# Reordering the head of a fused Fourier mixing and two-layer kernel: a forward piece, a table part, the layer weights and one copy

## Chip, core and metric

The kernel runs on one core of one Trainium2 chip. The metric is the device time of one execution in microseconds (us); 775.15 us is the median of three runs of the kernel before (773.96 to 775.66). The profile is of one further execution.

The engines are named as the profile names them: PE is TensorE (matmuls; PEld its weight loads), DVE is VectorE, ACT is ScalarE, POOL is GpSimd, SP is SyncE, which here only issues DMAs.

## What is computed

```python
def _attn_ref(x, filt_r, filt_i):            # x: (8, 3008, 256), filters: (1505, 256)
    X = np.fft.rfft(x, axis=1)
    F = (filt_r + 1j * filt_i)[None, :, :]
    y = np.fft.irfft(X * F, n=x.shape[1], axis=1)
    return y

def _moe_ref(x, w_in, w_out, alpha):         # x: (24064, 256), w_in: (256, 2048), w_out: (2048, 256)
    h = x @ w_in
    g = np.maximum(h, 0.0) + alpha * np.minimum(h, 0.0)
    return g @ w_out

def reference(x, filt_r, filt_i, w_in, w_out, alpha):
    y = _attn_ref(x, filt_r, filt_i)
    return _moe_ref(y.reshape(24064, 256), w_in, w_out, alpha)
```

Along the sequence each of the eight batches is filtered in the Fourier domain; then every token goes through two dense layers with a leaky activation whose slope differs by hidden unit.

## The kernel before

**Two halves woven together.** The length 3008 is split as 94 x 32. Each batch's transform is a chain of matmul stages (forward over 94, forward over 32, filter product, inverse over 32, inverse over 94) whose result is written to `yT`, channels on partitions and tokens along the free dimension. The dense layers work on blocks of 512 tokens (one of 384 in each pair of batches): `Block.up` multiplies `win_s` by `yT` into PSUM (L547), ScalarE copies it to `gtb` (L556), VectorE applies the activation (L559, L561), and `Block.down` multiplies by `wout_s` (L601). While the layers of one batch run, the transforms of the next are laid between them by a hand-written plan of steps. Sixteen steps make a block.

**The order is the program's.** The kernel's scheduling is manual: each engine takes its instructions in the order in which the code writes them, and an instruction that waits holds up all that stands behind it on its engine. The order around the change is therefore the order of the lines below.

**The first batch (class `First`, L412 to L512)** has nothing to run beside, so it has stages of its own, without trips through DRAM:

- `piece_a` (eight): forward over 94, into `am`.
- `turn_at(kp, n, evict)`, here "array piece kp": matmuls against the identity that transpose `am` into the array `at` for the products kp to kp + n - 1 (L343). They go to a bank pair of `psF` (or of `psH` with `wide`) and are copied out by the engine `evict` (the copies of all helpers on ScalarE and VectorE carry the lines L305 and L308).
- `piece_b(kp)`, twelve, the "forward pieces": 16 small matmuls (L355) of `twf_s` and `at` into a bank pair of `psH`, then one VectorE product with the filter (L360) into `uu`. Forward piece kp reads what the array piece that covers kp has left.
- `piece_c(kp)`, twelve: 16 matmuls (L382) of `uu` with the inverse tables `twi_s` and `twx_s` into two banks of `psO`; a pair of pieces shares the two banks. `keep_c` copies a pair out to `v` by ScalarE.
- `half_t`, `piece_t` (L399): transpose `v` into `zt`; `half_d`, `pair_d` (L283): the inverse over 94, into `psO` or `psF`, copied to `yT`. A `pair_d` fills a bank pair of `psF`.

**PSUM.** The pools `psH` and `psO` have two buffers each and `psF` has one (L77 to L79), so a stage that writes to `psF` waits until the last content of `psF` has been copied out.

**Tables.** `twf_s` comes in three parts of eight columns by SP's queue (`table`, L417; the second and third wait for a VectorE memset each). `inverse_table(ka, pb)` transposes one part with four matmuls (L421) into the bank `pb`, and ScalarE copies it to `twi_s`. `swapped(ka, eng)` makes `twx_s` from it (L428, L429): VectorE for part one, POOL for parts two and three. Pieces C 0 to 3 read part one, 4 to 7 part two, 8 to 11 part three.

**Warm matmuls.** `warm(n, pw)` issues n matmuls of 128x512 with the identity (L438) whose result nobody reads.

**Loads on POOL's queue.** The filters of the first batch (L140), in three groups, then the layer weights `win_s` (L482, two transfers) and `wout_s` (L485), with the inputs `xs` of the second batch between (L118). In front of the `win_s` load stands a VectorE memset of two of its columns (L480). The load waits for the memset, and the memset stands in VectorE's order behind the filter product of a certain piece; so its place in the loop sets when the load is issued.

**The first block (from L700)** runs in 16 steps: `up4(i, half)` in the even ones (L570: eight matmuls for four hidden groups and 256 tokens into one `psH` buffer; L578: ScalarE's copy; with half 1 also VectorE's activation L583, L584), and what is left of the first batch between, put into the plan step by step (L653 to L664). In step 0, `up4` also has the slopes of the activation and two copies done.

Of the kernel before, what the change touches and what calls it, by code (L numbers as in the profile page):

```python
# [51 lines left out]
def kernel(  # L52
# [10 lines left out]
    nc = tc.nc  # L63
# [48 lines left out]
    def load_x(b, c, held=False):  # L112
        xs = p_x.tile([128, 8 * D], FP16, name="xs")
        if held:
            for r in (slice(0, 32), slice(64, 96)):
                nc.vector.memset(xs[r, 0:2], 0.0)
        for r in (slice(0, 48), slice(48, N1)):
            nc.gpsimd.dma_start(out=xs[r], in_=xrow(b, c)[r])  # L118
        return xs
# [25 lines left out]
    def banks(wide):  # L145
        if wide:
            return psH.tile([128, 2, 512], FP32, name="hps")
        return psF.tile([128, 2, 512], FP32, name="psF")

    def bank(kind):  # L150
        if kind == "o":
            return psO.tile([128, 2, D], FP32, name="op").rearrange("p k d -> p (k d)")
        return banks(kind == "h")[:, 0]
# [150 lines left out]
    def on_act(o, i):  # L304
        nc.scalar.activation(o, i, AF.Copy)  # L305
# [113 lines left out]
    def inverse_table(ka, pb):  # L419
        for i in range(4):  # L420
            nc.tensor.matmul(pb[:, 128 * i : 128 * i + 128],  # L421
                             twf_s[:, ka + 2 * i : ka + 2 * i + 2].rearrange("p k m -> p (k m)"), id16,
                             start=True, stop=True)
        on_act(twi_s[:, ka : ka + 8].rearrange("p k m -> p (k m)"), pb)

    def swapped(ka, eng):
        t, o = twi_s[:, ka : ka + 8], twx_s[:, ka : ka + 8]
        eng.tensor_scalar(o[:, :, 32:64], t[:, :, 0:32], gs_s, None, OP.mult)  # L428
        eng.tensor_scalar(o[:, :, 0:32], t[:, :, 32:64], gs_s, -1.0, OP.mult, OP.mult)  # L429

    xc = {(0, c): load_x(0, c) for c in range(4)}
    f0 = First()
# [3 lines left out]
    def warm(n, pw):  # L436
        for _ in range(n):
            nc.tensor.matmul(pw.rearrange("p (r c) -> p r c", r=4), id16,  # L438
                             id16.unsqueeze(1).to_broadcast([128, 4, 128]), start=True, stop=True)
# [24 lines left out]
    swapped(8, nc.gpsimd)  # L464
    load_filt(nc.gpsimd, filt_s, 8, 12, (1,))
    f0.piece_b(1)
    warm(2, bank("o"))
    f0.turn_at(4, 2, on_act)
    nc.sync.dma_start(out=wi3_s, in_=consts["wi3"].ap())
    nc.sync.dma_start(out=al16, in_=moe_alpha.rearrange("(j p) -> j p", p=128))  # L470
# [3 lines left out]
    for r in (slice(0, 64), slice(64, 128)):  # L474
        nc.sync.dma_start(out=wfq_s[r], in_=consts["wfq"].ap()[r])
    for kp in range(12):
        if kp < 10:
            f0.piece_b(kp + 2)
        if kp == 5:
            nc.vector.memset(win_s[:, :, 0:1], 0.0)  # L480
            for kt in range(2):
                nc.gpsimd.dma_start(out=win_s[:, kt], in_=moe_w_in[kt * 128 : (kt + 1) * 128])  # L482
            xc[(1, 0)] = load_x(1, 0)
            for q in range(2):
                nc.gpsimd.dma_start(  # L485
                    out=wout_s[:, 8 * q : 8 * q + 8],
                    in_=moe_w_out[1024 * q : 1024 * q + 1024].rearrange("(j p) d -> p j d", p=128))
            for c in range(1, 4):
                xc[(1, c)] = load_x(1, c)
        f0.piece_c(kp)  # L490
        if kp > 9:
            f0.keep_c(kp, (on_act, on_act) if kp == 10 else both, 1)
        elif kp % 2 == 1:
            f0.keep_c(kp - 1, (on_act, on_act))
            if kp < 7:
                f0.turn_at(kp + 5, 2, on_act)
        if kp == 0:
            inverse_table(16, banks(False)[:, 0])
            swapped(16, nc.gpsimd)
        if 7 < kp < 10:  # L500
            warm(2, banks(False)[:, 0])
    for o in range(0, 128, 64):
# [109 lines left out]
    def put(step, fn, *args):  # L612
        plan.setdefault(step, []).append((fn, args))
# [42 lines left out]
    for i in (6, 7):  # L656
        put(3, lambda i=i: on_dve(*f0.half_t(i, "o")))
    put(5, f0.pair_d, 2, on_dve)
    put(9, f0.pair_d, 3, on_act)
    for g, ts, ds, te, de in ((2, (19, 23), (25, 28), (on_dve, on_dve), (on_dve, on_dve)),  # L660
                              (3, (32, 34), (43, 49), (on_act, on_act), (on_act, on_act))):
        for i in range(2):
# [102 lines left out]
```

## Time and profile before

| | |
|---|---|
| median of three runs | 775.15 us (773.96 to 775.66) |
| the profiled execution's own time | 773.89 us |
| its span, first to last instruction | 772.1 us |
| TensorE busy | 761.2 us, 99% |
| VectorE / ScalarE / POOL busy | 633.4 / 583.9 / 148.2 us |
| granted TensorE clock | 1.00 |
| DMA | 99.77 MB, mean 129 GB/s |

The profile's times are us from the span's start. A group's line reads: start, length, engine, line, operation, output<-input, shape, count, and in brackets the idle time of the engine before it with what ended it. Groups with a count span several instructions. TensorE by stretches:

| us | TensorE busy | what runs |
|---|---|---|
| 0 to 16 | 13.24 of 16.00 | loads, `piece_a`, warm matmuls |
| 16 to 20 | 3.56 of 4.00 | first array pieces and forward pieces |
| 20 to 27 | 6.59 of 7.00 | loop over the pieces, first half |
| 27 to 32 | 4.36 of 5.00 | loop, second half |
| 32 to 36.1 | 2.95 of 4.10 | last stages up to the first `yT`, start of the layer |
| 36.1 to 42 | 5.89 of 5.90 | first block, first part |
| 42 to 49 | 5.91 of 7.00 | first block, second part |
| 49 to 60 | 11.00 of 11.00 | second block with the second batch's transform |

Some matmul records can be missing from a trace, and the ends of matmuls are modelled.

### The profile page before, as it was taken

The page shows a single profiled execution, that of the slowest core. Times are in us where ns is not written, and L with a number is a line of the kernel's source. Part 1 is how long each engine was busy: PE and PEld are TensorE (multiplying, and loading weights), DVE is VectorE, ACT ScalarE, POOL GpSimd, SP SyncE. Part 2 cuts the span into 40 slices and gives each one's busy share as a digit, 9 for nine tenths or more (in the row PEclk, how much of TensorE's full clock was granted, in tenths as well). Part 3 has the DMA queues.
Part 4 walks back from the last instruction along what each step waited for, and adds up shares of the span by engine and source line. Part 5 has one row for each costly group of instructions (what it writes and reads, how often), then busy time and mean ns, then how long its engine had stood idle before and what let it go on. Part 6 is the DMA issues. An engine that isn't in the chain of part 4 may idle for free.

```text
span 772.1 us, 16602 instructions
## 1 busy us (share of the span) xinstructions
PE 761.2 (99%) x6552; PEld 510.5 (66%) x6552; DVE 633.4 (82%) x1159; ACT 583.9 (76%) x672; POOL 148.2 (19%) x278
## 2 busy tenths in 40 slices
PE   8899999999999999999999999999999999999998
PEld 4576656666666666666666666766666666766666
DVE  3788885889898998899978998899877888666663
ACT  3677788888778787887778878787777777676664
POOL 7620660132202212121201222022111112000000
PEclk9999999999999999999999999999999999999999
DMA  9896797674854548724783438644473233510111
GB/s 162 129 226 179 132 202 193 176 161 127 193 137 107 131 121 172 192 71 104 183 223 87 115 101 175 185 103 110 119 159 103 65 77 96 152 36 28 42 42 56
DMA packets 96814, 99.77 MB, mean 129 GB/s; under 512 B 12020, under 2 KB 83076, under 8 KB 96544
## 3 DMA queue, kind: packets, MB, share of 16 engines
q1 hardware_dynamic: 82048, 69.22, 32.5%
q0 software_dynamic: 14688, 29.49, 21.5%
q8 instruction: 51, 0.84, 0.5%
q14 instruction: 27, 0.22, 0.1%
HBM read 54.74 MB, written 46.66 MB: 131 GB/s over the span
## 4 chain that ended last, share of the span: by engine, by line
PE 95%; ACT 2%; DMA 1%; issue 1%; DVE 0%; POOL 0%; DVEq 0%; ACTq 0%
PE op L601 42%; PE hps L547 41%; PE psF L283 3%; PE hps L261 2%; PE psF L230 1%; PE op L438 1%; PE hps L176 1%; DMA win_s<-in_moe_w_in_dram 1%; PE hps L202 1%; ACT asb L305 1%; PE hps L570 1%; ACT gtb L578 1%; PE psF L399 0%; ACT gtb L556 0%; DVE uu L360 0%
## 5 line engine op out<-in xcount | busy, mean ns | idle before, releaser
L556 ACT ACTIVATE gtb<-hps 128x1024 f16<-128x1024 f32 (+1 forms) x376 | 377.4, 1006 | 134.7 <-PE hps L547 130.9
L601 PE MATMUL op<-wout_s,gtb 128*128 128x256 f16 x3008 | 431.3, 273 | 0.0
L547 PE MATMUL hps<-yT,win_s 128*128 128x512 f16 (+1 forms) x1504 | 418.4, 375 | 0.9 <-ACT asb L305 0.3
L601 PEld LDWEIGHTS <-gtb 128*128 128x128 f16 x3008 | 291.0, 98 | 164.2 <-issue 10.7
L559 DVE TENSOR_SCALAR m<-gtb,alm_s 128x512 f16<-128x512 f16 (+1 forms) x752 | 227.1, 345 | 99.6 <-ACT gtb L556 98.2
L561 DVE TENSOR_TENSOR gtb<-gtb,m 128x2048 f16<-128x2048 f16 (+1 forms) x188 | 226.1, 1203 | 10.3
L547 PEld LDWEIGHTS <-win_s 128*128 128x128 f16 x1504 | 142.6, 98 | 55.2 <-issue 6.6
L244 POOL DMA_DIRECT2D sw<-ww x144 | 71.6, 506 | 414.6 <-DVE ww L237 408.9
L606 ACT ACTIVATE osb<-op 128x512 f32<-128x512 f32 (+1 forms) x97 | 56.6, 584 | 12.4 <-PE op L601 11.3
L305 ACT ACTIVATE asb<-hps 128x1024 f16<-128x1024 f32 (+1 forms) x56 | 56.6, 1020 | 5.6 <-PE hps L176 4.3
L305 ACT ACTIVATE v<-hps 128x1024 f16<-128x1024 f32 (+1 forms) x43 | 43.4, 1010 | 10.8 <-PE hps L261 10.6
L237 DVE TENSOR_TENSOR ww<-psF,filts_s 128x1024 f16<-128x1024 f32 x42 | 51.2, 1218 | 0.2 <-PE psF L230 0.2
L238 DVE TENSOR_TENSOR uu<-psF,filt_s 128x1024 f16<-128x1024 f32 x42 | 51.0, 1215 | 0.0
L305 ACT ACTIVATE yT<-psF 128x752 f16<-128x752 f32 x59 | 46.9, 796 | 2.0 <-PE psF L283 1.9
L283 PEld LDWEIGHTS <-zt 96*128 96x128 f16 x512 | 28.6, 98 | 6.0 <-issue 0.3
L283 PE MATMUL psF<-wi_s,zt 96*128 96x94 f16 x496 | 31.0, 205 | 0.1
L242 POOL DMA_DIRECT2D uu<-ww x24 | 19.6, 1255 | 32.7 <-DVE uu L238 24.7
L249 DVE TENSOR_TENSOR uu<-uu,sw 128x1024 f16<-128x1024 f16 x36 | 24.6, 683 | 1.2 <-DMA sw<-ww 0.9
L118 POOL DMA_DIRECT2D xs<-in_x_dram x32 | 21.6, 889 | 13.1 <-PE hps L547 4.8
L186 DVE TENSOR_TENSOR xs<-xs 47x2048 f16<-47x2048 f16 x16 | 19.5, 1219 | 0.4
L190 DVE TENSOR_TENSOR xs<-xs 47x2048 f16<-47x2048 f16 x16 | 19.4, 1210 | 0.0
L261 PE MATMUL hps<-uu,twi_s 64*64 64x256 f16 x336 | 17.3, 281 | 0.0
(88 smaller groups left out, 264.4 us busy)
## 6 DMA issues: line engine op xcount, KB each, us to landing
out_dram<-osb SPq DMA_DIRECT2D x128, 128.0 KB
v_dram<-v SPq DMA_DIRECT2D x84, 128.0 KB
zt<-v_dram SPq DMA_DIRECT2D x28, 384.0 KB
sw<-ww POOLq DMA_DIRECT2D x144, 64.0 KB, 2.8
xs<-in_x_dram POOLq DMA_DIRECT2D x44, 192.0 KB, 6.4
at<-a_dram SPq DMA_DIRECT2D x40, 192.0 KB
a_dram<-asb SPq DMA_DIRECT2D x32, 192.0 KB
a_dram<-asb SPq DMA_DIRECT2D x12, 384.0 KB
```

The lines of the kernel that those rows point to most:

```text
L237: nc.vector.tensor_mul(ww, px, fs)
L238: nc.vector.tensor_mul(uu, px, f)
L244: nc.gpsimd.dma_start(out=sw[o : o + 32], in_=ww[i : i + 32])
L261: nc.tensor.matmul(ps[64 * par : 64 * par + 64, e, 256 * h : 256 * h + 256], twi_s[r, 4 * q + 2 * h + par], u[r, par, h], start=True, stop ...
L283: nc.tensor.matmul(ps[:, m], self.zt[:, 8 * g + 4 * mh + m, dh * 128 : dh * 128 + 128], wi3_s, start=True, stop=True)
L305: nc.scalar.activation(o, i, AF.Copy)
L547: nc.tensor.matmul(self.hps[:, j % 2, 0:tn], win_s[:, kt, j * 128 : (j + 1) * 128], yT[:, kt, self.t0 : self.t0 + tn], start=(kt == 0), st ...
L556: nc.scalar.activation(g[:, 2 * i : 2 * i + 2], self.hps[:, :, 0:tn], AF.Copy)
L559: nc.vector.tensor_scalar(m[:, 2 * i + h], g[:, 2 * i + h], 0.0, a, OP.min, OP.mult)
L561: nc.vector.tensor_add(g, g, m)
L601: nc.tensor.matmul(self.op[:, si - s0], self.gts[k][:, 128 * si : 128 * si + 128], wout_s[:, k], start=(si == s0 and k == 0), stop=(si == ...
L606: nc.scalar.activation(osb[:, 0:m], self.op[:, 0:m], AF.Copy)
```

## The change

Four places, all in the first 50 us.

- In the head, the two warm matmuls behind forward piece 1 are taken out. In their place stand `inverse_table` and `swapped` for table part three, with a bank of `psO` in place of one of `psF`, and then forward piece 2. Array piece 4 follows these. In the loop, piece 2 and the table part are taken out.
- In the loop, the memset and the six POOL loads behind it (two of `win_s`, `xs`, `wout_s`, `xs`) stand in round 4 in place of round 5: behind forward piece 6, not 7.
- `pair_d` 3 of the first batch stands in step 7 in place of step 9, and VectorE copies it in place of ScalarE.

```diff
@@ -464,7 +464,9 @@
     swapped(8, nc.gpsimd)
     load_filt(nc.gpsimd, filt_s, 8, 12, (1,))
     f0.piece_b(1)
-    warm(2, bank("o"))
+    inverse_table(16, bank("o"))
+    swapped(16, nc.gpsimd)
+    f0.piece_b(2)
     f0.turn_at(4, 2, on_act)
     nc.sync.dma_start(out=wi3_s, in_=consts["wi3"].ap())
     nc.sync.dma_start(out=al16, in_=moe_alpha.rearrange("(j p) -> j p", p=128))
@@ -474,9 +476,9 @@
     for kp in range(12):
-        if kp < 10:
+        if 0 < kp < 10:
             f0.piece_b(kp + 2)
-        if kp == 5:
+        if kp == 4:
             nc.vector.memset(win_s[:, :, 0:1], 0.0)
             for kt in range(2):
                 nc.gpsimd.dma_start(out=win_s[:, kt], in_=moe_w_in[kt * 128 : (kt + 1) * 128])
@@ -494,9 +496,6 @@
             f0.keep_c(kp - 1, (on_act, on_act))
             if kp < 7:
                 f0.turn_at(kp + 5, 2, on_act)
-        if kp == 0:
-            inverse_table(16, banks(False)[:, 0])
-            swapped(16, nc.gpsimd)
         if 7 < kp < 10:
             warm(2, banks(False)[:, 0])
@@ -656,7 +655,7 @@
     put(5, f0.pair_d, 2, on_dve)
-    put(9, f0.pair_d, 3, on_act)
+    put(7, f0.pair_d, 3, on_dve)
```

## The prediction

> **What bounds the kernel now.** I read four views in this order. First the page's busy table, and TensorE's waits over the whole span, longest total first (us in total, times, longest):
>
> ```profile
> PE 761.2 (99%) x6552; PEld 510.5 (66%) x6552; DVE 633.4 (82%) x1159; ACT 583.9 (76%) x672; POOL 148.2 (19%) x278
> ...
> PE hps L570 <- DMA win_s<-in_moe_w_in_dram: 0.8, 1, 0.8
> PE hps L570 <- ACT gtb L578: 0.6, 1, 0.6
> ...
> PE psF L421 <- ACT at L305: 0.4, 1, 0.4
> PE hps L570 <- ACT yT L305: 0.4, 1, 0.4
> ```
>
> TensorE is busy 761.2 of 772.1 us. Split by window, this view lists only two waits after 80 us, 0.2 us each (a PSUM copy near 117 us, another near 149), and the stretch 49 to 60 has 11.00 of 11.00 us busy. So from 49 us on the time is TensorE's own work, and a microsecond saved before that should come off the end whole. All four edits act before 49 us.
>
> Second, the chain of waits over the first 60 us (start, length, what):
>
> ```profile
> 18.96 1.03 ACT at L305
> ...
> 20.03 0.38 PE psF L421 x4
> ...
> 27.07 0.43 POOL win_s L482
> ...
> 27.66 8.41 DMA win_s<-in_moe_w_in_dram
> ...
> 36.11 0.94 PE hps L570 x7
> ```
>
> The chain runs through an array copy by ScalarE, the third table part, the filter products (L360), then the load of `win_s`, which VectorE's memset releases. It lands at 36.06 and the first layer product goes on at 36.11.
>
> Third, VectorE in order of time, which shows how products and memset stand:
>
> ```profile
> 16.72 2.36 DVE L360 TENSOR_TENSOR uu<-hps,filt_s 128x1024 f16<-128x1024 f32 x2 [0.21 <-DMA filt_s<-in_filt_r_dram]
> 19.34 1.22 DVE L360 TENSOR_TENSOR uu<-hps,filt_s 128x1024 f16<-128x1024 f32 x1 [0.26 <-PE hps L355]
> 20.83 7.05 DVE L360 TENSOR_TENSOR uu<-hps,filt_s 128x1024 f16<-128x1024 f32 x6 [0.27 <-PE hps L355]
> 26.70 0.06 DVE L480 MEMSET win_s<- 128x2 f16 x1
> ```
>
> Products 0 and 1 end at 19.08; VectorE then idles 0.26 us for piece 2 and 0.27 for piece 3. Products 4 to 7 start at 22.12, 23.26, 24.39 and 25.55 by the chain: 1.15 us apart.
>
> Fourth, TensorE around the start of the layer:
>
> ```profile
> 35.09 0.27 PE L570 MATMUL hps<-yT,win_s 128*128 128x256 f16 x1 [0.41 <-ACT yT L305]
> 36.11 0.94 PE L570 MATMUL hps<-yT,win_s 128*128 128x256 f16 x7 [0.76 <-DMA win_s<-in_moe_w_in_dram]
> ```
>
> Without the load's wait the second matmul would follow the first by its 0.11 to 0.13 us, at 35.20. So the load costs 36.11 - 35.20 = 0.91 us, and whatever is gained beyond that must come from the FFT chain that makes `yT` ready at 35.09.
>
> **Piece 2 and table part 3 moved.** Removed from the head: the two warm matmuls at 17.70 (0.54 us of TensorE). In their place stand the table's four (0.22 us, row at 20.03), to 17.92. Piece 2 reads what the array copy of 17.24 to 18.26 leaves, so it cannot start before about 18.31 (it was 18.85); its 16 matmuls take 0.34. Array piece 4 follows at 18.65, 0.34 later than before, its copy from 19.30 to 20.33 instead of 18.96 to 19.98. ScalarE's table copy (0.60) now stands ahead of it, from 18.68 to 19.28, in time in which ScalarE waits for array piece 4 anyway; without that cover it would add its 0.6 to the array copy. Two things wait on these copies. Piece C 0 needs both `psO` banks, and the second is now the table's: free at 19.28, so C 0 at 19.33 (19.20 before). Array piece 6 needs `psF`, free at 20.33.
>
> From there: piece 3 at 19.70 instead of 20.35, because the 0.43 us wait for `psF` and the table's 0.32 have left the loop. Product 2 follows product 1 directly (19.08), product 3 starts at 20.25 (20.83 before), array piece 6 at 20.38, piece 4 at 20.95, product 4 at 21.37 against 22.12: 0.75 us sooner. The loop behind (C, copies of C, array piece) keeps its 2.25 us per pair, within VectorE's 2.3. I take 0.7 sooner for the whole FFT chain; the bounds are 0.26 (only the idle before product 2 goes) and 0.75. Filters don't hold it: those for products 4 to 7 were issued by 17.09 and landed within 4.6 us, r parts by 18.9 and i parts by 20.1; the last ones, for 8 to 11, landed at 25.5 (issued 23.0, 2.5 us), and product 8 would start at about 26.0. POOL's order is unchanged: the swapped copy of part 3 stays behind the last filter issue, 23.60 to 24.99, and layer weights come next. SP's queue is not touched.
>
> Is part 3 of `twf_s` there at 17.7? The trace shows its issue at 13.00 and a first reader at 20.03 that waited for ScalarE, not for it. SP's queue has by its packet count (81,664 left at 13.0 us, 81,338 at 15.5; 256 are the two last table parts) moved it by 15.5. So landing lies between 15.5 and 20.03. I take the early end, no cost; the late end is a rival below.
>
> **Layer weights one product sooner.** The memset moves from behind product 7 to behind product 6: 1.15 us. With the 0.75 of product 4 it comes at 24.80 instead of 26.70. POOL finishes its swapped copy at 24.99 and then issues six transfers, `win_s` first: 25.2 instead of 27.07. The DMA rows say 0.10 busy share in 25 to 26 and 0.00 in 26 to 28, so the load meets nothing, and takes its 9.0 us from issue to landing: 34.2. Lower bound, from one product alone: 36.06 - 1.15 = 34.91. The issues of `xs` and `wout_s` behind it shift with it; each is wanted later (`wout_s` at 47.2).
>
> First layer matmul: 35.09 - 0.7 = 34.4, the second at 34.5, the load at 34.2 no longer last. Gain: 36.11 - 34.5 = **1.6 us**, of which 0.9 is the load and 0.7 the FFT. Bounds: 36.06 - 34.91 = 1.15 if the load stays last, 0.91 + 0.26 = 1.17 if the FFT hardly moves, 0.91 + 0.75 = 1.66 at best.
>
> **One copy on VectorE, a step earlier.** In the chain:
>
> ```profile
> 42.28 1.94 ACT gtb L578 x2
> 44.21 0.69 ACT yT L305
> 44.90 0.93 ACT gtb L578
> ```
>
> ScalarE loses 0.69 there. But pair 3 now stands ahead of the layer's fifth product, and its bank `psF` is free only when VectorE has copied pair 2, at 42.34. Times of before: pair 3 at 42.39 to 42.80, fifth product until 43.7, its copy from 43.75 instead of 43.22: 0.53 given back, so 0.16 left, of which I take 0.1. On VectorE the copy (0.94, as pair 2) falls into an idle stretch of 1.90 us before 44.25; what is late next is the activation of the first chunk, by 0.53, and VectorE then runs without idle until 58.7. The nearest consumer is pair 4, which TensorE starts at 59.41 and which needs VectorE's copy ending at 58.67: 0.7 us of slack, just enough. Bounds: +0.69 saved to 0.55 lost.
>
> **Sum.** 1.6 + 0.1 = 1.7 us off. The profiled execution was 773.89 us (span 772.1 and 1.8 around it), so 772.2; it lies 1.26 below the median shown, and from the median 775.15 I forecast **773.45 us**, 0.22% less. Own range of this case: 1.2 to 2.4 off.
>
> **Rivals.** (1) Load or FFT moves only half way: 0.9 to 1.2 off, **774.1**. For it: piece 2 still waits for an array copy, and slacks in the loop (piece 4 ends 21.3, VectorE wants it 21.35) are near nothing. Against: no new wait is longer than the one removed. 11%. (2) VectorE becomes the bound from 44 us: 0.55 lost instead of 0.1 gained, 1.6 - 0.55 = 1.05 off, **774.1**. For: no idle until 58.7. Against: the 0.7 of slack. 8%. (3) Table part 3 lands late, at its bound of 20.03. TensorE stops at the head of its queue, with piece 2, array piece 4 and C 0 behind it; product 2 then starts at 20.66, product 4 at 23.3, 1.2 later than before, and the layer at 36.3: 0.3 slower, **775.4**. Against: the packet count. 4%. (4) The other side: the TensorE clock. The warm matmuls leave a hole of 0.4 us at 17.9. If the granted clock fell to half from there for about 4 us, the 3.56 us of work that the rows show busy in 16 to 20 would take as much again; TensorE would be last in the loop, 3.6 - 1.7 = 1.9 us more than before, **777.0**. It decides from a mean clock below about 0.7 in that stretch. Against: 1.00 in every row, also in 32.0 to 36.1, where TensorE is busy only 2.95 of 4.10 us. 13%, with whatever else I have not seen on that side.
>
> [...]
>
> **How the numbers follow.** Forecast 64%. About 0.2% (1.55 us) is what a measurement of this kernel can tell from no change; the forecast's 1.7 is barely beyond it, and I put 57 of its 64 there and 7 within. Rivals 1 to 3 fall within (23). So faster 0.57, same 0.30, slower 0.13. The range holds the forecast and rivals 1 to 3 and the spread of runs (773.96 to 775.66, 0.85 to each side): 772.3 to 775.9; it leaves rival 4 out.
>
> **What would show it.** Right: no idle before product 2; product 4 near 21.4; memset near 24.8 and `win_s` issued near 25.2; first two layer matmuls 0.1 apart near 34.4; the block's first L547 at 47.2 instead of 48.92; span 770.4. Wrong: TensorE waiting at 17.7 for `twf_s`; a wait for the load still there; clock below 1.00 in 16 to 22; a new wait for VectorE near 57 us; or the lead at 49 us lost again later.

## The result

The changed kernel takes 772.56 us (median of seven runs, 772.30 to 773.03) against 775.15 us (seven runs, 773.96 to 775.66): a ratio of 0.9972, 95% interval 0.996 to 0.9983, or 2.59 us at the medians. The profiled execution took 772.30 us with a span of 770.5 us, 1.6 us less than the span of before. The forecast was 773.45 us with a span of 770.4.

TensorE's waits after the change, longest total first, without the one for the very first load (us in total, times, longest). Lines behind the change carry numbers one lower than before: L569 is the first block's layer product, L546 that of the later blocks.

```profile
PE hps L546 <- ACT asb L305: 0.5, 2, 0.3
PE hps L569 <- ACT yT L305: 0.4, 1, 0.4
...
PE hps L569 <- ACT gtb L577: 0.2, 1, 0.2
PE hps L355 <- ACT at L305: 0.2, 1, 0.2
```

The wait for `win_s` (0.8) and the wait for `psF` ahead of the table (0.4) are gone; the one for ScalarE's layer copies fell from 0.6 to 0.2. New are three waits of 0.2 each: of forward piece 2 for the array copy, of a later forward piece for a product, and of pair 3 for VectorE's copy of pair 2.

VectorE and POOL after the change, groups in order of time:

```profile
16.84 9.16 DVE L360 TENSOR_TENSOR uu<-hps,filt_s 128x1024 f16<-128x1024 f32 x8 [0.49 <-DMA filt_s<-in_filt_r_dram]
24.81 0.06 DVE L482 MEMSET win_s<- 128x2 f16 x1
```

```profile
25.18 1.14 POOL L484 DMA_DIRECT2D win_s<-in_moe_w_in_dram  x2 [0.61 <-DVE win_s L482]
```

The first eight products now run without a hole; memset and load stand 1.9 us earlier than before (26.70 and 27.07).

TensorE after the change:

```profile
17.55 0.40 PE L421 MATMUL op<-ids,twf_s 128*128 128x128 f16 x4
18.16 0.41 PE L355 MATMUL hps<-at,twf_s 64*32 64x256 f16 x16 [0.22 <-ACT at L305]
...
34.20 1.16 PE L569 MATMUL hps<-yT,win_s 128*128 128x256 f16 x8 [0.40 <-ACT yT L305]
...
47.15 1.02 PE L546 MATMUL hps<-yT,win_s 128*128 128x512 f16 x4 [0.32 <-ACT asb L305]
```

All eight matmuls of the first layer product are one group: in this execution nothing waits for the weights. (In the profiles of f2 and g4 below, which have the same order of loads, a wait of 0.20 and 0.23 us is left, so the load still lands close to the moment at which it is wanted.) The second block starts at 47.15 instead of 48.92, 1.77 us sooner; the span shows 1.6 of it, and where the other 0.17 went is told below.

### The profile page after: what moved, and what is told of

It is laid out like the page before. It is cut to its first block, busy times and chain, and to the rows that moved or that the text cites. A ratio compares the mean times of both kernels' runs of the same rounds, so it can differ in the third digit from the quotient of the medians.

```text
span 770.5 us, 16598 instructions
## 1 busy us (share of the span) xinstructions
PE 760.9 (99%) x6550; PEld 510.2 (66%) x6550; DVE 634.2 (82%) x1160; ACT 583.2 (76%) x671; POOL 147.9 (19%) x278
## 3 DMA queue, kind: packets, MB, share of 16 engines
q0 software_dynamic: 14688, 29.49, 21.4%
## 4 chain that ended last, share of the span: by engine, by line
PE 96%; ACT 3%; issue 0%; DVE 0%; DMA 0%; ACTq 0%
PE op L600 42%; PE hps L546 41%; PE psF L283 3%; PE hps L261 2%; PE psF L230 1%; PE hps L176 1%; PE op L438 1%; PE hps L202 1%; ACT asb L305 1%; PE hps L569 1%; ACT v L305 1%; PE op L382 1%; PE psF L399 0%; ACT gtb L577 0%; ACT gtb L555 0%; PE hps L355 0%
## 5 line engine op out<-in xcount | busy, mean ns | idle before, releaser
L546 PE MATMUL hps<-yT,win_s 128*128 128x512 f16 (+1 forms) x1504 | 418.4, 375 | 0.9 <-ACT asb L305 0.5
L546 PEld LDWEIGHTS <-win_s 128*128 128x128 f16 x1504 | 142.5, 98 | 55.2 <-issue 6.6
```

Source lines behind the costliest of these rows:

```text
L546: nc.tensor.matmul(self.hps[:, j % 2, 0:tn], win_s[:, kt, j * 128 : (j + 1) * 128], yT[:, kt, self.t0 : self.t0 + tn], start=(kt == 0), st ...
```

## The experiments

Two things were open. Which part brings how much; and why the medians moved by 2.6 us where the two profiles differ by 1.6. The runs of before lie in two groups, 774.0 to 774.2 and 775.1 to 775.7, those after the change in one. Each run below has a mean granted TensorE clock on record; the tables count the runs at 0.998 or less, and the others are called undisturbed. Kernels named e were run on one chip, those named f on a second, those named g on a third, each set beside 33 runs of the kernel before on its own chip.

**Each part alone, and the change without its last part.**

```diff
 e1_head_only: of the change, only
+    inverse_table(16, bank("o")); swapped(16, nc.gpsimd); f0.piece_b(2)    # for warm(2, ...)
 e2_weights_only: of the change, only
-        if kp == 5:
+        if kp == 4:
 e3_copy_only: of the change, only
-    put(9, f0.pair_d, 3, on_act)
+    put(7, f0.pair_d, 3, on_dve)
 e4_no_copy: the change, but for e3's line
```

> Only piece 2 and table part 3 are moved; the layer weights stay behind product 7, pair 3 stays on ScalarE in step 9. Theory (the later of two ends sets the layer's start: yT from the FFT chain, or the load of the weights): the FFT chain alone makes the first layer matmul start at 34.2 (35.09 before), but product 7 ends near 26.0, so the weights are issued near 26.3 and land near 35.3; TensorE waits about 1.0 us for them, and 0.75 us of the 1.6 us of span is gained: span 771.3. Rival A (the weights' earlier issue is worth nothing by itself, the FFT chain brings all): no wait for the load, span 770.5. Rival B (the spread of the runs before, 773.96 to 775.66 in two groups 1.3 us apart, comes from the load's landing while it is last): this kernel still waits for the load, so its runs keep a spread above 1 us; if the spread comes from the head of the FFT instead, its runs lie within 0.8 us as those after the change do.

> Only the memset and the loads behind it are moved from product 7 to product 6; the head stays as before, pair 3 stays on ScalarE in step 9. Theory: weights issued 1.1 us sooner, near 25.95, landing near 34.95; first layer matmul stays at 35.09 and the second follows it at once, so 0.9 us is gained at the layer's start: span 771.2, and TensorE's wait for the load is gone. Rival A: the span stays at 772.1 because the load takes longer when it starts earlier. Rival B (spread from the load's landing): runs within 0.8 us, median below 774.2.

> Only pair 3 is moved to step 7 and copied by VectorE. Theory: of the 0.69 us that ScalarE saves about 0.53 is given back, since the fifth layer product now stands behind pair 3, which waits for its PSUM bank: 0.1 to 0.2 us sooner at the start of the second block (48.7 to 48.8, 48.92 before), span 771.9 to 772.0. Rival A: ScalarE's 0.69 come off whole, 48.2 and span 771.4. Rival B: VectorE becomes the bound, a wait for VectorE at 47 to 59 us and span 772.4 or more.

> The change without its last part: pair 3 stays in step 9 on ScalarE. Theory: the layer starts at 34.2 as after the change, the second block 0.1 us later than after it (47.25 against 47.15), span 770.6. Rival A: 0.5 to 0.7 us later (47.7 or more, span 771.1), if the copy on ScalarE costs more once the layer starts sooner. Rival B: sooner than after the change, if the copy's move only costs.

| kernel | runs | of them with clock 0.998 or less | median us | median of the others | ratio, 95% interval |
|---|---|---|---|---|---|
| before | 33 | 16 | 774.71 | 774.17 | |
| e1_head_only | 11 | 6 | 774.77 | 773.57 | 0.9999, 0.9988 to 1.0009 |
| e2_weights_only | 11 | 0 | 773.15 | 773.15 | 0.9976, 0.9967 to 0.9984 |
| e3_copy_only | 11 | 5 | 774.57 | 774.38 | 0.9998, 0.9988 to 1.0008 |
| e4_no_copy | 11 | 5 | 772.97 | 772.50 | 0.9987, 0.9976 to 0.9999 |

The groups are groups by clock. Where the weights come sooner alone, no run has the lower clock, and nearly the whole gain of the medians is there: 1.56 us, against 1.74 in e4, which has the head as well. The head and the copy alone measure as no change. Among undisturbed runs the head is worth more: 0.60 us alone (five runs, 0.75 expected) and 0.65 beside the weights (773.15 to 772.50); in e4 the runs with the lower clock give most of that back at the median. The profile of e1_head_only has a stretch at half clock. Windows of it (us, then busy us and count of TensorE, its weight loads, VectorE, ScalarE and POOL, granted clock, DMA share, GB/s):

```profile
33.69:37.10 3.41, 2.01 (x22) 1.29 (x20) 1.31 (x3) 1.27 (x3) 0.84 (x2) 1.00 1.17 195
37.10:40.50 3.40, 3.40 (x28) 2.92 (x26) 1.94 (x3) 1.39 (x3) 1.13 (x3) 0.51 1.45 198
40.50:44.00 3.50, 3.50 (x42) 3.14 (x41) 2.23 (x3) 2.61 (x3) 0.63 (x2) 0.99 1.18 217
```

The wait for the load (1.0 us here) and the one for `yT` (0.4) leave TensorE 2.01 of 3.41 us busy; then it runs at half clock for 3.4 us, in the first block, where it is the bound. The profile of e3_copy_only shows the same from 37.7 to 41.1. That suggests that my reading in the expectations, by which the spread comes from the load's landing time, missed the means, and that the wait brings the clock down; f3 below tests it.

For e2_weights_only, the chain of waits shows the first layer product in one piece:

```profile
34.64 1.16 PE hps L570 x8
```

Weights issued at 25.48 (25.95 expected), no wait for them, span 770.9 (771.2 expected). In this profile product 0 began 0.45 us sooner than in that of before (16.27 against 16.72), for which the edit isn't the reason, so the profile's lead is partly luck; the run medians are the better measure.

The profile of e4_no_copy has a half-clock stretch elsewhere. TensorE in order of time, and windows of it:

```profile
17.56 0.40 PE L421 MATMUL op<-ids,twf_s 128*128 128x128 f16 x4 [0.33 <-DMA twf_s<-c_twf]
19.10 0.41 PE L355 MATMUL hps<-at,twf_s 64*32 64x256 f16 x16 [1.14 <-DVE uu L360]
```

```profile
16.60:20.00 3.40, 1.93 (x52) 1.08 (x49) 2.18 (x2) 2.01 (x3) 2.02 (x5) 1.00 0.91 126
20.00:23.40 3.40, 3.40 (x84) 2.21 (x84) 2.55 (x4) 2.71 (x4) 3.27 (x6) 0.51 0.57 74
```

Here the first filters landed late: product 0 began at 17.82 us, not at 16.7, and forward piece 2, which waits for the bank that product 0 frees, stood in TensorE's queue for 1.14 us; table part 3 was 0.33 us late as well. The layer then began at 36.11. In the order of before the same wait is shorter at the same landing: in the profile of f4 below, with product 0 at 17.79, it is 0.31 us. That raised the question whether the moved head invites the half clock.

**The changed kernel again, and the clock tested.**

```diff
 f1_after_again: the changed kernel
 f2_warm_in_hole: the changed kernel, with
+    hole = bank("o")
+    warm(2, hole)
-    inverse_table(16, bank("o"))
+    inverse_table(16, hole)
 f3_filled_wait: the kernel before, with
     f0.half_d(2, on_dve, "o")
+    warm(4, bank("o"))
 f4_no_warm: the kernel before, with
     f0.piece_b(1)
-    warm(2, bank("o"))
```

> The changed kernel itself, once more, beside the kernel before. What is open: about half of the runs of the kernel before, of the head alone and of the copy alone show a mean clock of 0.998 and are 1.2 us longer; their profiles show 3.4 us at half clock after the wait for the layer weights (37 to 41 us). Theory (the wait brings the half clock, so taking the wait away takes it away there): no half-clock stretch behind 34 us here; median 772.5 to 772.9, against 774.7 before. Rival (the moved head brings a half-clock stretch of its own, at 20 to 23.5 us, in the runs in which the first filters land late, as in the profile of the change without the copy): 3 to 6 of 11 runs have a mean clock of 0.998 or less and lie 1.5 to 2 us above the others, and the median moves to 773 to 774.5.

> The changed kernel with the two warm matmuls back in the hole behind forward piece 1, in the bank that the table part overwrites next. Theory: they fill 0.4 us that TensorE waits anyway, so in a clean run nothing changes by more than 0.1 us (span 770.5). If the half clock at 20 us of the moved head is due to the warm matmuls taken out, fewer runs than of the changed kernel show a mean clock of 0.998 or less (at most 1 of 11). Rival (it is due to the late filters, which stop VectorE and so TensorE for longer than 0.4 us): as many runs as of the changed kernel.

> The kernel before with four warm matmuls (0.87 us) in TensorE's wait for the layer weights, between the last stage's first two pieces and the first layer product; nothing else is changed. Clock theory: the wait itself stays (span of a clean run 772.1), but TensorE is busy in it, so the 3.4 us at half clock behind it are gone: all runs at 0.999 to 1.000, median 774.0 to 774.2 against 774.7 before, and a spread below 1.2 us. Rival (the spread comes from when the load lands, not from the clock): the same two groups of runs as before, median 774.7.

> The kernel before without the two warm matmuls behind forward piece 1; nothing else is changed. By the step of the prediction that costed their removal at nothing, the span stays at 772.1 and as many runs as before (about half) have a clock of 0.998. Rival (they hold up the clock): a half-clock stretch near 20 us in some runs, more runs at 0.998 or less than of the kernel before, mean clock down to 0.996 where both stretches fall in one run, median 1 us or more above.

| kernel | runs | of them with clock 0.998 or less | median us | median of the others | ratio, 95% interval |
|---|---|---|---|---|---|
| before | 33 | 18 | 774.66 | 774.06 | |
| f1_after_again | 9 | 0 | 772.95 | 772.95 | 0.9978, 0.9969 to 0.9987 |
| f2_warm_in_hole | 11 | 0 | 772.93 | 772.93 | 0.9974, 0.9966 to 0.9983 |
| f3_filled_wait | 11 | 0 | 774.17 | 774.17 | 0.9993, 0.9985 to 1.0002 |
| f4_no_warm | 12 | 4 | 774.17 | 773.85 | 0.9995, 0.9987 to 1.0004 |

f3_filled_wait leaves the cause of the stretch behind the load's wait with little doubt. TensorE in its profile, at the start of the layer:

```profile
36.11 1.02 PE L438 MATMUL op<-ids 128*128 128x512 f16 x4 [0.40 <-ACT yT L305]
36.97 1.04 PE L571 MATMUL hps<-yT,win_s 128*128 128x256 f16 x8
```

The warm matmuls do nothing but occupy TensorE up to the first layer product, which then runs without a wait. The runs lie where undisturbed runs of before lie (774.17 against 774.06), and none of the eleven has a lower clock, against 18 of 33. (The ratio's interval still reaches 1.0002; it is the group that tells, not the ratio.) So in these runs the half clock at the start of the layer goes with TensorE standing idle at the load (0.76 us in the profile of before). The changed kernel shows no lower clock in 7 and 9 runs, and e2 none in 11: without the wait the stretch behind it is gone. Its lead over the medians, 1.71 us here, is then 1.11 between undisturbed runs and 0.60 of half clock avoided.

For the two warm matmuls that the change removed no effect is seen: without them (f4) no more runs show the lower clock (4 of 12), and with them back (f2) the median stays within 0.02 us. In f2's profile the load is once more the last thing that the layer waits for, if briefly:

```profile
35.30 0.94 PE L571 MATMUL hps<-yT,win_s 128*128 128x256 f16 x7 [0.20 <-DMA win_s<-in_moe_w_in_dram]
```

**Late filters on purpose, and the order in the head.**

```diff
 g1_late_before: the kernel before; g2_late_after: the changed kernel, both with
+    load_filt(nc.gpsimd, filt_s, 8, 9, (0,))
     load_filt(nc.gpsimd, filt_s, 0, 4)
 g4_order: the changed kernel, with the order
     f0.turn_at(4, 2, on_act)
     f0.piece_b(2)
 g3_late_order: both edits
```

> The kernel before with the first filters made late on purpose: four small filter loads (of the last group, loaded again later with the same values) stand ahead of the first group on POOL's queue. The profiles so far show product 0 anywhere from 16.3 to 18.1 us by how late those filters land. What is open: whether the order of the moved head (forward piece 2, which waits for the bank that product 0 frees, now ahead of array piece 4) turns a late filter into a longer hole in TensorE. Theory: product 0 1 to 2 us later, near 18 to 19; in the order of before TensorE still has the warm matmuls and array piece 4 to do (1.1 us) ahead of the waiting piece, so its hole is product 0's end less 18.9. The load of the layer weights stays last or nearly so; the runs with a mean clock of 0.998 or less stay about as many as before (half), from the wait at 36 us. Rival (the order plays no part): the same hole as in the next kernel.

> The changed kernel with the same late filters. Theory: the hole begins near 17.9 instead of 18.9 and so is about 0.8 to 1.0 us longer than in the kernel before with late filters, TensorE busy about 2.0 to 2.5 of 4 us in 17 to 21; in some runs the clock is then halved for 3.4 us near 20 to 24 us (mean clock 0.998 or less, those runs 1.5 to 2 us longer). Rival (the order plays no part; the half clock of the profile without the copy was chance): no run below 0.999, and the same lead over its late counterpart as in the undisturbed pair, 1.6 to 1.8 us.

> The changed kernel with the same late filters and with array piece 4 ahead of forward piece 2 again; the table part stays where the change put it. Theory: array piece 4 (0.55 us) runs inside the hole, which is that much shorter than in the kernel just above, and its copy is done sooner; so fewer half-clock runs and, with late filters, the same time or up to 0.5 us less in clean runs. Rival: no difference, since product 0's end sets all that follows.

> The changed kernel with array piece 4 ahead of forward piece 2 again, filters as they are. Theory: in a run with early filters forward piece 2 comes 0.5 us later (18.85) and VectorE idles 0.26 us ahead of product 2 as before the change, but the table's place already brings most of the gain; the loop behind is paced by ScalarE's copies, so 0 to 0.3 us is lost against the change: median 772.6 to 773.3. Rival: forward piece 2's move is what counts, and 0.6 us or more of the gain is lost (773.5 or more).

| kernel | runs | of them with clock 0.998 or less | median us | median of the others | ratio, 95% interval |
|---|---|---|---|---|---|
| before | 33 | 13 | 774.14 | 773.87 | |
| g1_late_before | 11 | 8 | 776.39 | 775.34 | 1.0027, 1.0018 to 1.0036 |
| g2_late_after | 11 | 4 | 775.01 | 774.28 | 1.0006, 0.9996 to 1.0016 |
| g3_late_order | 11 | 6 | 774.88 | 774.60 | 1.0010, 1.0001 to 1.0019 |
| g4_order | 11 | 0 | 772.89 | 772.89 | 0.9978, 0.9970 to 0.9987 |

With late filters the lower clock comes to the changed kernel too (4 of 11), and to the kernel before in 8 of 11; where it lies is seen in one profile only, that of g2 (20.2 to 27.1 us).

The order of piece 2 and array piece 4 does change the hole. In the profile of g2 forward piece 2 waits 2.70 us for product 0, which began at 19.77; in those of g3 and g1 the wait is 0.90 and 0.75 us, with product 0 at 18.69 and 18.49. Of these differences 1.1 to 1.3 us are the later product 0 itself and about 0.7 us the order, and e4 against f4 above gives 0.83 at nearly the same product 0. But in the times the order doesn't tell: 4 and 6 of 11 runs at the lower clock, medians 0.13 us apart. So the first half of my theory (the longer hole) is borne out, the second (more half clock, more time) is not.

With filters as they are, piece 2 behind array piece 4 (g4) leads its kernel before by 0.98 us between undisturbed runs; the changed kernel leads by 1.11 on another chip (f1). The 0.13 between them is less than such a comparison can tell, and the 0.26 at which I had costed piece 2's move lies within the same noise. In g4's profile product 0 began at 17.34, where, as shown below, there is little for the head to gain. How much of the head's gain is the table part's and how much piece 2's therefore stays open. Also open is why five of eleven runs of e4_no_copy had a lower clock, and none of sixteen of the changed kernel nor of the 22 of f2 and g4: e4 was not run on the same chip as these, and in its profile the half clock lies in the head (20.0 to 23.4 us), which all of them share but for the order in g4 and the warm matmuls in f2.

g1_late_before shows what late filters do to the head's gain, and f4 that they need not be made late on purpose. VectorE in their profiles, g1 first:

```profile
18.49 9.14 DVE L360 TENSOR_TENSOR uu<-hps,filt_s 128x1024 f16<-128x1024 f32 x8 [1.89 <-DMA filt_s<-in_filt_r_dram]
```

```profile
17.79 6.88 DVE L360 TENSOR_TENSOR uu<-hps,filt_s 128x1024 f16<-128x1024 f32 x6 [1.45 <-DMA filt_s<-in_filt_r_dram]
```

Both have the order of before in the head, and yet the products run without a hole: when product 0 is late, TensorE has got ahead and VectorE's chain of products is the bound by itself. The profiles without a half-clock stretch (us; from the profiles' rows; f3 is left out, because its product 8 waited 1.38 us for its filters):

| kernel | product 0 | weights issued | layer's second matmul | second block | second block less product 0 |
|---|---|---|---|---|---|
| before | 16.72 | 27.07 | 36.11 | 48.92 | 32.20 |
| f4_no_warm | 17.79 | 27.25 | 35.88 | 48.69 | 30.90 |
| g1_late_before | 18.49 | 27.96 | 36.84 | 49.66 | 31.17 |
| e2_weights_only | 16.27 | 25.48 | 34.75 | 47.68 | 31.41 |
| after | 16.84 | 25.18 | 34.31 | 47.15 | 30.31 |
| f1_after_again | 17.32 | 25.66 | 34.96 | 47.80 | 30.48 |
| f2_warm_in_hole | 17.59 | 25.93 | 35.30 | 48.03 | 30.44 |
| g4_order | 17.34 | 25.79 | 35.23 | 47.97 | 30.63 |
| g3_late_order | 18.69 | 27.02 | 36.26 | 49.10 | 30.41 |

(Where the first layer product is one group, its second matmul is taken 0.11 us behind its start.) With product 0 at 16.3 to 16.8 the weights bring 0.79 (32.20 - 31.41) and head and copy 1.10 more (31.41 - 30.31). With product 0 near 17.7 all together bring 0.46 (30.90 - 30.44), and near 18.6 they bring 0.76 (31.17 - 30.41): no more than the weights alone, so by these pairs nothing is left for the head. Each of these figures is from one pair of profiles.

**What the copy costs at the far end.** In every profile in which VectorE copies pair 3 (after, e3, f1, f2, g2, g3, g4) VectorE stands 0.46 to 0.47 us ahead of the last block's last activation; in those with the copy on ScalarE (before, e1, e2, e4, f3, f4, g1) it doesn't. Before and after, in order of time:

```profile
761.84 0.61 DVE L559 TENSOR_SCALAR m<-gtb,alm_s 128x512 f16<-128x512 f16 x2 [1.00 <-ACT gtb L556]
762.56 1.23 DVE L561 TENSOR_TENSOR gtb<-gtb,m 128x2048 f16<-128x2048 f16 x1
```

```profile
760.08 0.62 DVE L558 TENSOR_SCALAR m<-gtb,alm_s 128x512 f16<-128x512 f16 x2 [1.00 <-ACT gtb L555]
761.15 1.23 DVE L560 TENSOR_TENSOR gtb<-gtb,m 128x2048 f16<-128x2048 f16 x1 [0.46 <-DVE m L558]
```

TensorE's last 72 matmuls, in the chain of waits after the change:

```profile
758.98 3.49 PE op L600 x32
762.48 0.04 issue
762.52 4.54 PE op L600 x40
```

Before, the chain has them in one piece of 7.88 us; here they take 8.07 with the gap, 0.19 more, which is about the 0.17 that the span lacks. What VectorE waits for isn't in the trace. Its program has one instruction more in just these kernels (1160 instead of 1159); whether that is the cause was not tested.

## Why the prediction was right, and where not

**What bounds: right.** From 47 us on TensorE runs as before, and a gain at the head comes off the end, but for those 0.17 us. That the span came out at 770.5 against 770.4 is partly luck, though, since errors cancel: the layer's second matmul came 1.80 us sooner (36.11 to 34.31), more than the 1.6 forecast and than the 1.66 "at best"; then 0.03 was lost up to the second block, where 0.1 was to be gained, and 0.17 at the end.

**Weights one product sooner: right.** Memset at 24.81 (24.80 forecast), issue at 25.18 (25.2), no wait in this profile. POOL had its swapped copy done by 24.57, not 24.99, and stood 0.61 us for the memset, which alone set the issue. e2 shows the 0.9 by itself: 1.02 between undisturbed medians, 0.79 in the profiles.

**Head: right in kind in this profile, its size taken for more certain than it is.** Product 4 came at about 21.4 as forecast (16.84 and four products of 1.15). The first layer matmul came at 34.20 (34.4), 0.89 sooner than before, which is more than the upper bound of 0.75; the last product ended 0.90 sooner too (31.57 to 30.67). The working went only as far as product 4 and so did not cover the rest of the loop, where before also waits 0.19 ahead of its last product. But "I take 0.7 sooner for the whole FFT chain" took product 0's start as given. It follows the landing of the first filters, from 16.3 to 18.1 us where these were not delayed on purpose, and the later it is, the less is left of the head's gain: from 17.8 on it is about nothing (f4, g1). The lower bound of 0.26 should have been zero. That product 0 began early in both profiles compared (16.72 and 16.84) was luck. Piece 2's start had a second condition that the prediction left out: it waits for the bank that product 0 frees, 0.85 us in the profile of f1. f1's undisturbed lead of 1.11 us lies where rival 1 (half the gain) put it, but not for the reasons that rival 1 gave.

**Copy on VectorE: right at its place, wrong over the whole.** From the layer's second matmul to the second block it takes 12.84 us with the copy on VectorE (after, f1) and 12.93 without (e2; e4, 49.15 - 36.22), where no wait for the load precedes: 0.09 gained, 0.1 forecast. The cause of its smallness is as forecast in kind: pair 3, which now stands ahead of the fifth product, waits 0.2 us for its bank. Where the wait for the load precedes, the same stretch takes 12.81 us with the copy on ScalarE (before); so about 0.1 of the 0.91 that I put on the wait is given back behind it. The 0.17 at the end is more than the copy gains; e3 measures as no change. The 0.7 us of slack in front of pair 4 held: there is no wait for VectorE near 57 us.

**Rival 3, a late table part,** occurs in small: 0.33 us in the profile of e4, 0.6 with late filters in g2; never the 2.3 us later than 17.7 that the rival took as its bound. The packet count, by which the part had landed by 15.5 in the profile of before, does not carry over to these two executions: there TensorE waited for it until 17.56 and 17.95.

**The clock, rival 4: right in kind, wrong in place and sign.** I looked for the half clock in the 0.4 us hole of the head and dismissed it by "1.00 in every row, also in 32.0 to 36.1". That row was one execution. (That the hole itself costs nothing, as the sum had it, was my estimate; without the warm matmuls, f4 has 4 of 12 runs at the lower clock against 18 of 33 of before, and with them back the median of f2 stays within 0.02 us.) In about half of the other executions (47 of 99 runs beside the experiments) the mean clock is 0.998 or less. No profile of such a run of the kernel before was kept, but those of e1 and e3 show the half clock right behind that very stretch, with its wait for the load, and f3, with the wait filled, shows no lower clock; the change takes the wait away. So the term that the sum lacked is half clock avoided: 0.6 us at the medians of f1, and 1 us in the first comparison, where the median run of before, by its time, had it (its clock is not on record; 2.59 against 1.6 in the profiles). The measured 772.56 thus lies 0.89 below the forecast for a reason that the prediction did not have.

## What to carry to other kernels

Here a wait of about one microsecond on a TensorE-bound path (0.8 in the profile of before, 1.0 in those of e1 and e3) cost more than itself, in some executions only: the runs of before with the lower clock took 1.27 to 1.30 us more at the median than its others (775.44 against 774.17, 775.33 against 774.06 and 775.17 against 773.87 us, one pair for each chip). So compare the mean clock of many runs, not one profile, before "the clock is 1.00" is used as an argument, and test it by filling the wait with matmuls nobody reads. A step's gain holds only while the chain that it shortens is the last; say what starts that chain, here a filter load whose landing moves by almost 2 us (product 0 from 16.27 us in e2 to 18.06 in e3), and cost the step at both ends of it. The part that looks least (one condition moved by one round) can carry most of the measured gain.

## What the runs showed of the hardware that was not expected

The granted clock went to half (0.50 to 0.51) for 3.4 us in three profiles (37.1 to 40.5 in e1, 37.7 to 41.1 in e3, 20.0 to 23.4 in e4) and for 6.9 us, twice that, in the profile of g2 (20.2 to 27.1). In the 3.41 us ahead of it TensorE was busy 2.01, 2.01, 1.94 and 0.97 us; in e1 that is 59% busy, with single holes of 0.4 and 1.0 us. Other profiles have 3.41 us with as little, 1.91 in g3 (from 17.8) and 1.67 in f3 (from 26.0), or a little more, 2.25 in before (from 33.0), and show 1.00 throughout. So the busy time alone does not tell in these profiles whether the half clock comes. What decides which executions have it, about half of those of before (47 of 99 runs at 0.998 or less), was not shown.
